# The launch of a linear-attention and MLP kernel: load order of a weight piece and an activation tile, and the place of that tile's statistics

## Chip, core and metric

One NeuronCore of a Trainium2 chip runs the whole program. The metric is the device time of one execution in microseconds; smaller is better.

## What is computed

Two identical layers on a sequence of 2048 rows of 448 features, all in float32. Each layer is an attention block without softmax and a GELU block, each behind a layer norm without gain:

```
x = x + A(layernorm(x));  x = x + B(layernorm(x))      # twice
A: q, k, v = split(x @ wqkv)        # 448 -> 3 * 448, 16 heads of 28
   phi(t) = where(t > 0, t + 1, exp(t)) + 1e-6
   kv = sum_s phi(k)[s] v[s]^T ;  z = sum_s phi(k)[s]
   o = (phi(q) kv) / (phi(q) . z + 1e-6) ;  return o @ wo
B: gelu(x @ w1 + b1) @ w2 + b2      # 448 -> 1792 -> 448
```

The change touches only the start of the first layer's attention: the layer norm of the first two tiles of x and their product with the part of wqkv that makes k.

## The kernel before

The 2048 rows are 16 tiles of 128 rows; four tiles make a block. The 448 features are cut into chunks of 128, 128, 128 and 64. Float32 products are made of two parts in the faster float32r form: each operand is a rounded `hi` and a remainder `lo`, and a product is hi·hi + hi·lo + lo·hi (L307 to L309 for a 128-row chunk, L311 and L312 for the last one, where hi and lo of the weight lie on top of one another in one piece).

A weight piece comes from HBM to a staging tile (`stage_piece`, L91, L93, L94), ScalarE (ACT) casts it to `hi` (`split_hi`, L127), and VectorE (DVE) or GpSimd (POOL) subtracts to get `lo` (`split_lo`, L134, L137). POOL does it for pieces 1 and 2 of wk and 0 and 2 of wq, DVE for the others.

A tile of x goes through these steps:

- `load_x` (L82): a DMA of 224 KB on SyncE's queue (SP).
- `stage_a`, which is `ln_stats` (L197 to L205): DVE makes the statistics (`bn_stats` L194, `bn_aggr` L200, add of epsilon L202), POOL takes the power -1/2 (L204, tile `brs`). `ln_bn` (L192) is the first of these alone.
- `stage_n` (L381): DVE normalises the tile in place (L384), and ACT copies its last 64 columns, doubled, to a tile `tail` (L388).
- `stage_b`: TensorE (PE) transposes the four chunks into one PSUM tile `tp` (L247); the fourth reads `tail`.
- For tiles 0 and 1 the split of the transposed tile is made in halves of 256 columns (`split_half`): ACT casts `XH` (L260), DVE subtracts `XL` (L262). Half 0 holds chunks 0 and 1, half 1 holds chunks 2 and 3. Half 0 of `XL` waits until both casts of `XH` are done.

The program is in a fixed order that is written by hand (`manual_schedule`): each engine takes its own instructions in the order in which the program issues them, and a waiting instruction holds up those behind it on its engine. For the start, that order is the code at L144 to L159, the calls at L912 to L919, and the string `LAUNCH` (L520), whose tokens `launch` (L534) takes one after the other: `ka1` is the cast of wk's piece 1, `kb1` its remainder, `ha0`/`hb0` the two casts of `XH` of tile 0, `la0`/`lb0` the two remainders `XL`, `n1` the normalisation of tile 1, `T1` its transposes, `K01` the products of tile 0 with wk's piece 1, `a2` the statistics of tile 2, and `Q..` the same as `K..` for wq.

On PE the launch is in this order: 11 warming products of a tile of ones (L157, each recorded as two), the transposes of tile 0, two more warming products, K00, T1, K01, K10, K11, K02, K12, K03, K13, and the same for q. On POOL, after the constants, it is: power of tile 0, power of tile 1, remainder of wk's piece 1, of piece 2, of wq's pieces 0 and 2. On SP it is: tile 0, tile 1, pieces 0 to 3 of wk (piece 3 in two halves of 112 KB), pieces 0 to 2 of wq, tile 2, piece 3 of wq, tiles 3 and on. There are eight DMA semaphores in turn, so that from the ninth DMA on SP waits for the landing of the DMA eight places ahead.

The calls before the loop over layers are, in the kernel before (L912 to L919):

```python
stage_a(0, 0)
bn = ln_bn(xt[0, 1])
stage_n(0, 0)
split_hi("k", 0, st_k)
sts[0, 1] = ln_stats(xt.pop((0, 1)), bn)
stage_b(0, 0)
warm_up(2)
```

Behind the launch comes the rest of layer 0's pass over the 16 tiles, then the product of the attention state with wv and wo, then the MLP over four blocks beside the q side of the next block, and the same for layer 1.

Of the kernel before, what the change touches and what calls it, by code (L numbers as in the profile page):

```python
# [22 lines left out]
def linear_attn_mlp_kernel(  # L23
# [15 lines left out]
    S, D = x0.shape  # L39
# [27 lines left out]
    def t448(tag, bufs, name, dt=F32):  # L67
        bufs = NH if tag == "H" else bufs
        return work.tile([128, D], dt, name=name, tag=tag, bufs=bufs)
# [8 lines left out]
    xt = {}  # L78

    def load_x(l, t):  # L80
        xt[l, t] = t448("H", 8, f"x{l}_{t}")
        sp.dma_start(xt[l, t], x_d[l][t * 128:(t + 1) * 128, :])  # L82
# [5 lines left out]
    def stage_piece(src, c, eng, s):  # L88

        if c < 3:  # L90
            eng.dma_start(s, src[c * 128:(c + 1) * 128, :])  # L91
        else:
            eng.dma_start(s[0:64], src[TL:D, :])  # L93
            eng.dma_start(s[64:128], src[TL:D, :])  # L94
        return s

    def load_kq(col, st, cs):
        src = wqkv[:, col:col + D]
        for c in cs:
            if c % 2 == 0:  # L100
                st.append(work.tile([128, 1024], F32, name="stg", tag="S", bufs=5))
                st.append(st[-1][:, 512:512 + D])
                st[-2] = st[-2][:, :D]
            stage_piece(src, c, sp, st[c])
        return st

    def stage_square(src):

        st = []
        for h in range(2):  # L110
            s = work.tile([128, 1024], F32, name="stg", tag="S", bufs=5)[:, :2 * D]
            s = s.rearrange("p (c n) -> p c n", c=2)
            if h == 0:
                sp.dma_start(s, src[:256, :].rearrange("(c p) n -> p c n", p=128))
            else:
                sp.dma_start(s[:, 0], src[256:TL, :])
                sp.dma_start(s[:64, 1], src[TL:, :])
                sp.dma_start(s[64:, 1], src[TL:, :])
            st += [s[:, 0], s[:, 1]]
        return st  # L120

    def piece(name, i):
        return t448(f"{'W' if name == 'k' else 'V'}{i}", 1, f"w{name}{i}", F32R)

    def split_hi(name, c, st):
        hi = piece(name, c if c < 3 else 6)
        act.copy(hi, st[c])  # L127
        wkq[name, c] = (hi, piece(name, 3 + c)) if c < 3 else hi

    def split_lo(name, c, st, eng):  # L130

        if c < 3:
            hi, lo = wkq[name, c]
            eng.tensor_tensor(lo, st[c], f(hi), op=OP.subtract)  # L134
        else:
            lo = wkq[name, 3][64:128]
            eng.tensor_tensor(lo, st[c][64:128], f(lo), op=OP.subtract)  # L137

    def split_kq(name, st):
        for c in range(4):  # L140
            split_hi(name, c, st)
            split_lo(name, c, st, pool if c in ((1, 2) if name == "k" else (0, 2)) else dve)

    load_x(0, 1)  # L144
    st_k = load_kq(D, [], range(4))
    st_q = load_kq(0, [], range(3))
    load_x(0, 2)
    load_kq(0, st_q, (3,))
# [6 lines left out]
    def warm_up(n):  # L155
        for i in range(n):
            pe.matmul(warm[:, :128], ones, ones, start=True, stop=True)  # L157
# [34 lines left out]
    def ln_bn(xs):  # L192
        st = work.tile([128, 6], F32, name="bst", tag="bst", bufs=3)
        dve.bn_stats(st, xs)  # L194
        return st

    def ln_stats(xs, st=None):  # L197
        st = ln_bn(xs) if st is None else st
        mv = work.tile([128, 2], F32, name="bmv", tag="bmv", bufs=3)
        dve.bn_aggr(mv, st)  # L200
        ve = work.tile([128, 1], F32, name="bve", tag="bve", bufs=3)
        dve.tensor_scalar(ve, mv[:, 1:2], 1e-5, None, op0=OP.add)  # L202
        rs = work.tile([128, 1], F32, name="brs", tag="brs", bufs=3)
        pool.tensor_tensor(rs, ve, mhalf, op=OP.pow)  # L204
        return xs, mv, rs  # L205
# [166 lines left out]
    sts = {}  # L372
# [8 lines left out]
    def stage_n(l, t):  # L381

        xs, mv, rs = sts.pop((l, t))
        dve.tensor_scalar(xs, xs, mv[:, 0:1], rs, op0=OP.subtract, op1=OP.mult)  # L384
        xns[l, t] = xs
        if t < TURNED[l]:
            d = tails[l, t] = work.tile([128, 128], F32, name="tail", tag="tail", bufs=2)
            act.copy(d.rearrange("p (u n) -> p u n", u=2), xs[:, None, TL:].to_broadcast([128, 2, 64]))  # L388
# [12 lines left out]
    def stage_b(l, t, tag="h"):  # L401
        if t < TURNED[l]:
            transpose_x(xns[l, t], tails.pop((l, t)), ("a", l, t // 4), t % 4, tag)
# [72 lines left out]
    def stage_g(l, t, acc):  # L476
# [41 lines left out]


    LAUNCH = (  # L520
        "kb0 ha0 hb0 ka1 kb1 la0 n1 lb0 K00 T1 K01 ha1 hb1 la1 lb1 ka2 kb2 K10 K11 ka3 kb3 qa0 qb0 K02 K12 K03 K13 "
        "qa1 qb1 qa2 qb2 Q00 Q10 Q01 Q11 Q02 Q12 s0 a2 kp0 qa3 qb3 kh0 n2 kl0 kp1 Q03 Q13"
    )
    PRE = 5
# [386 lines left out]

    stage_a(0, 0)  # L912
    work.tile([128, 32], F32, name="space", tag="space", bufs=1)
    bn = ln_bn(xt[0, 1])
    stage_n(0, 0)
    split_hi("k", 0, st_k)
    sts[0, 1] = ln_stats(xt.pop((0, 1)), bn)
    stage_b(0, 0)
    warm_up(2)  # L919

    for l in range(LAYERS):
        tr = SimpleNamespace(mp={})
# [34 lines left out]
        for b in range(NB):  # L957
            acc = [bank("acc", 4, f"y{j}")[:, :D] for j in range(4)]
            nxt = b + 1 < NB
            if not nxt and l + 1 < LAYERS:  # L960
                st_k = stage_square(wqkv[:, D:2 * D])
# [58 lines left out]
```

## Time and profile before

| what | us |
|---|---|
| median of 3 runs | 878.07 |
| lowest, highest | 877.53, 878.48 |
| the profiled execution | 878.62 |
| its span, first to last instruction | 876.9 |

The profiled execution is about 0.6 us above the median, and 1.7 us of it lie outside the span. In the rows of the timeline, the first number is the start in us from the span's start, the second the time that the instruction took; then come engine, line, operation, the tiles written and read, and in brackets the idle time of the engine before it with what ended it. PE's weight loads have an engine name of their own (PEld). A matmul's end is modelled and lies later than the start of the next one, so that PE's pace is read from start to start.

### The profile page before, as it was taken

The page shows a single profiled execution, that of the slowest core. Times are in us where ns is not written, and L with a number is a line of the kernel's source. Part 1 is how long each engine was busy: PE and PEld are TensorE (multiplying, and loading weights), DVE is VectorE, ACT ScalarE, POOL GpSimd, SP SyncE. Part 2 cuts the span into 40 slices and gives each one's busy share as a digit, 9 for nine tenths or more (in the row PEclk, how much of TensorE's full clock was granted, in tenths as well). Part 3 has the DMA queues.
Part 4 walks back from the last instruction along what each step waited for, and adds up shares of the span by engine and source line. Part 5 has one row for each costly group of instructions (what it writes and reads, how often), then busy time and mean ns, then how long its engine had stood idle before and what let it go on. Part 6 is the DMA issues. An engine that isn't in the chain of part 4 may idle for free.

```text
span 876.9 us, 11676 instructions
## 1 busy us (share of the span) xinstructions
PE 870.9 (99%) x4182; PEld 771.9 (88%) x4182; DVE 489.9 (56%) x953; ACT 343.5 (39%) x603; POOL 220.9 (25%) x250
## 2 busy tenths in 40 slices
PE   9999999999999999999999999999999999999998
PEld 8989888888888888888899998888888888888887
DVE  6878585658455443226467875864674473433112
ACT  5677635324223322333355665332233133223221
POOL 5566532335012102011222344120220140140000
PEclk9999999999999999999999999999999999999999
DMA  5475636623313402051145443262332413111001
GB/s 158 133 227 166 208 88 203 191 87 131 132 59 104 156 0 97 1 179 49 48 136 186 168 131 106 98 186 81 106 112 91 132 69 118 49 49 41 2 1 43
DMA packets 63482, 94.76 MB, mean 108 GB/s; under 512 B 8896, under 2 KB 58560, under 8 KB 63424
## 3 DMA queue, kind: packets, MB, share of 16 engines
q1 hardware_dynamic: 63424, 94.01, 33.5%
q8 instruction: 33, 0.54, 0.3%
q14 instruction: 25, 0.20, 0.1%
HBM read 56.17 MB, written 34.60 MB: 104 GB/s over the span
## 4 chain that ended last, share of the span: by engine, by line
PE 97%; DMA 1%; DVE 0%; POOL 0%; SPq 0%; issue 0%; ACT 0%; POOLq 0%; DVEq 0%
PE y L822 10%; PE y L820 10%; PE y L821 10%; PE hp L803 9%; PE hp L804 9%; PE hp L802 9%; PE hp L806 3%; PE hp L805 3%; PE psq L307 2%; PE psk L308 2%; PE psq L309 2%; PE psq L308 2%; PE psk L309 2%; PE G L483 2%; PE psk L307 2%; PE G L482 2%
## 5 line engine op out<-in xcount | busy, mean ns | idle before, releaser
L812 DVE TENSOR_TENSOR gl<-g,gh 128x512 fp32r<-128x512 f32 x112 | 83.1, 742 | 300.7 <-ACT gh L811 300.7
L808 ACT ACTIVATE g<-hp,b1s 128x512 f32<-128x512 f32 x112 | 77.2, 689 | 406.2 <-PE hp L806 402.7
L822 PE MATMUL y<-w2h,gl 128*128 128x448 f32 x448 | 163.7, 365 | 0.0
L821 PE MATMUL y<-w2l,gh 128*128 128x448 f32 x448 | 163.6, 365 | 0.0
L820 PE MATMUL y<-w2h,gh 128*128 128x448 f32 x448 | 163.6, 365 | 0.0
L803 PE MATMUL hp<-XH,w1l 128*128 128x512 f32 x336 | 131.5, 392 | 0.0
L802 PE MATMUL hp<-XH,w1h 128*128 128x512 f32 x336 | 131.2, 391 | 0.0
L804 PE MATMUL hp<-XL,w1h 128*128 128x512 f32 x336 | 131.2, 391 | 0.0
L204 POOL TENSOR_TENSOR brs<-bve,mhalf 128x1 f32<-128x1 f32 x64 | 39.5, 618 | 283.8 <-DVE bve L202 280.7
L820 PEld LDWEIGHTS y<-w2h,gh 128*128 128x128 f32 x448 | 84.1, 188 | 9.0
L821 PEld LDWEIGHTS y<-w2l,gh 128*128 128x128 f32 x448 | 84.1, 188 | 8.4
L822 PEld LDWEIGHTS y<-w2h,gl 128*128 128x128 f32 x448 | 84.2, 188 | 6.6
L804 PEld LDWEIGHTS hp<-XL,w1h 128*128 128x128 f32 x336 | 63.1, 188 | 14.1 <-issue 0.6
L803 PEld LDWEIGHTS hp<-XH,w1l 128*128 128x128 f32 x336 | 63.1, 188 | 11.3
L802 PEld LDWEIGHTS hp<-XH,w1h 128*128 128x128 f32 x336 | 63.1, 188 | 10.9
L811 ACT CAST gh<-g 128x512 fp32r<-128x512 f32 x112 | 69.6, 622 | 3.6
L695 POOL TENSOR_TENSOR pz<-pq,zb 128x448 f32<-128x448 f32 x32 | 36.7, 1150 | 86.4 <-DVE dn L701 75.5
L417 POOL TENSOR_TENSOR xnl<-x,xnh 128x384 fp32r<-128x384 f32 x32 | 35.1, 1097 | 70.8 <-ACT xnh L416 38.8
L297 DVE TENSOR_TENSOR XL<-sp,XH 128x512 fp32r<-128x512 f32 x50 | 44.4, 894 | 3.8 <-ACT XH L296 3.8
L806 PE MATMUL hp<-XL,w1x 128*128 128x512 f32 x112 | 43.6, 389 | 0.0
L805 PE MATMUL hp<-XH,w1x 128*128 128x512 f32 x112 | 43.6, 389 | 0.0
L764 POOL TENSOR_TENSOR x<-x,b2b 128x448 f32<-128x448 f32 x32 | 41.9, 1332 | 0.0
(146 smaller groups left out, 1563.9 us busy)
## 6 DMA issues: line engine op xcount, KB each, us to landing
x<-in_A_x_dram SPq DMA_DIRECT2D x32, 224.0 KB, 3.6
pq_d<-eq SPq DMA_DIRECT2D x32, 224.0 KB, 2.9
pq<-pq_d SPq DMA_DIRECT2D x32, 224.0 KB, 3.2
sq_m<-sq SPq DMA_DIRECT2D x14, 512.0 KB, 2.8
sp<-sq_m SPq DMA_DIRECT2D x56, 128.0 KB, 2.8
x<-x_d SPq DMA_DIRECT2D x32, 224.0 KB, 3.3
sq_a<-sq SPq DMA_DIRECT2D x12, 512.0 KB, 2.9
sp<-sq_a SPq DMA_DIRECT2D x48, 128.0 KB, 3.1
```

Source lines behind the costliest of these rows:

```text
L297: eng.tensor_tensor(lo.rearrange("p (c i n) -> p c i n", c=4, n=32), x, f(h), op=OP.subtract)
L802: pe.matmul(o, w1h[:, c, s], x.moving(x.hi, c), start=(c == 0), stop=False)
L803: pe.matmul(o, w1l[:, c, s], x.moving(x.hi, c), start=False, stop=False)
L804: pe.matmul(o, w1h[:, c, s], x.moving(x.lo, c), start=False, stop=False)
L805: pe.matmul(o, w1x[:, s], x.moving(x.hi, 3), start=False, stop=False)
L806: pe.matmul(o, w1x[:, s], x.moving(x.lo, 3), start=False, stop=True)
L808: act.activation(g, hp, AF.Gelu_apprx_tanh, bias=b1s[:, i:i + 1])
L811: act.copy(gh, g)
L812: dve.tensor_sub(gl, g, f(gh))
L820: pe.matmul(acc[j], gh[:, s], w2h[:, i], start=first, stop=False)
L821: pe.matmul(acc[j], gh[:, s], w2l[:, i], start=False, stop=False)
L822: pe.matmul(acc[j], gl[:, s], w2h[:, i], start=False, stop=last)
```

## The change

Three edits.

1. Load order on SP: tile 0, then wk's piece 0, then tile 1, then wk's pieces 1 to 3; the rest as before.
2. Before the loop, the cast of wk's piece 0 stands ahead of tile 0's normalisation with its copy of the tail. On ACT the order becomes: cast of piece 0, `tail` of tile 0, both halves of `XH`, cast of piece 1 and so on as before. The statistics of tile 1 leave this place; in `LAUNCH` they come back as `a1`, behind `la0`. On DVE the order becomes: statistics of tile 0, its normalisation, remainder of wk's piece 0, half 0 of `XL`, the three instructions of tile 1's statistics, half 1 of `XL`, normalisation of tile 1. On POOL nothing changes places: the power of tile 1 is still ahead of the remainder of wk's piece 1.
3. The two warming products behind tile 0's transposes are removed. PE's order is otherwise the same.

In `LAUNCH`, `ka1 kb1` move behind `lb0`, which changes no engine's order except as told above.

```diff
+    st_k = load_kq(D, [], range(1))
     load_x(0, 1)
-    st_k = load_kq(D, [], range(4))
+    load_kq(D, st_k, range(1, 4))
     st_q = load_kq(0, [], range(3))
...
     LAUNCH = (
-        "kb0 ha0 hb0 ka1 kb1 la0 n1 lb0 K00 T1 K01 ha1 hb1 la1 lb1 ka2 kb2 K10 K11 ka3 kb3 qa0 qb0 K02 K12 K03 K13 "
+        "kb0 ha0 hb0 la0 a1 lb0 ka1 kb1 n1 K00 T1 K01 ha1 hb1 la1 lb1 ka2 kb2 K10 K11 ka3 kb3 qa0 qb0 K02 K12 K03 K13 "
...
     stage_a(0, 0)
     work.tile([128, 32], F32, name="space", tag="space", bufs=1)
-    bn = ln_bn(xt[0, 1])
+    split_hi("k", 0, st_k)
     stage_n(0, 0)
-    split_hi("k", 0, st_k)
-    sts[0, 1] = ln_stats(xt.pop((0, 1)), bn)
     stage_b(0, 0)
-    warm_up(2)
```

## Prediction

> **What bounds the kernel now.** I read the page first, then PE's waits over the whole span, then the timeline of the launch. The page's busy shares:
>
> ```profile
> PE 870.9 (99%) x4182; PEld 771.9 (88%) x4182; DVE 489.9 (56%) x953; ACT 343.5 (39%) x603; POOL 220.9 (25%) x250
> ```
>
> PE never rests outside a few places, so a change at the start can only move the moment from which PE runs without gaps. PE's waits name those places:
>
> ```profile
> PE warm L157 <- DVE ones L152: 1.1, 1, 1.1
> PE psq L307 <- DVE eq L321: 0.5, 1, 0.5
> PE psk L307 <- ACT XH L260: 0.5, 1, 0.5
> ```
>
> The first and the third lie in the launch. The second is late:
>
> ```profile
> 47.64 0.47 PE L307 MATMUL psq<-wq,XH 128*128 128x448 f32 x1 [0.48 <-DVE eq L321]
> ```
>
> It belongs to tiles that are loaded and split long after the launch, by engines that are themselves led by PE; I let it move along with the rest, and keep its 0.48 as the most that it could give back. Now the launch:
>
> ```profile
> 0.80 0.86 SPq L82 DMA_DIRECT2D x<-in_A_x_dram  x2
> ...
> 1.70 1.38 SPq L91 DMA_DIRECT2D stg<-in_A_wqkv_dram  x3
> ...
> 3.42 0.63 DVE L194 BATCH_NORM_STATS2 bst<-x 128x6 f32<-128x448 f32 x1 [2.35 <-DMA x<-in_A_x_dram]
> ...
> 4.37 0.62 DVE L194 BATCH_NORM_STATS2 bst<-x 128x6 f32<-128x448 f32 x1
> 4.53 0.55 POOL L204 TENSOR_TENSOR brs<-bve,mhalf 128x1 f32<-128x1 f32 x1 [2.17 <-DVE bve L202]
> 5.12 0.51 DVE L384 TENSOR_SCALAR x<-x,bmv,brs 128x448 f32<-128x448 f32 x1
> ...
> 5.66 0.30 ACT L388 COPY tail<-x 128x128 f32<-128x128 f32 x1 [3.58 <-DVE x L384]
> ...
> 6.16 0.27 PE L247 MATMUL tp<-ident,tail 128*128 128x128 f32 x1
> ...
> 6.44 0.56 ACT L127 CAST wk<-stg 128x448 fp32r<-128x448 f32 x1 [0.48 <-DMA stg<-in_A_wqkv_dram]
> 6.91 0.64 ACT L260 CAST XH<-tp 128x256 fp32r<-128x256 f32 x2
> ...
> 7.33 0.47 PE L307 MATMUL psk<-wk,XH 128*128 128x448 f32 x1 [0.45 <-ACT XH L260]
> 7.44 0.58 ACT L127 CAST wk<-stg 128x448 fp32r<-128x448 f32 x1
> 7.58 0.42 DVE L262 TENSOR_TENSOR XL<-tp,XH 128x256 fp32r<-128x256 f32 x1
> ...
> 7.92 0.50 DVE L384 TENSOR_SCALAR x<-x,bmv,brs 128x448 f32<-128x448 f32 x1
> ...
> 8.10 1.33 POOL L134 TENSOR_TENSOR wk<-stg,wk 128x448 fp32r<-128x448 f32 x1 [1.55 <-ACT wk L127]
> ...
> 8.46 0.30 ACT L388 COPY tail<-x 128x128 f32<-128x128 f32 x1 [0.45 <-DVE x L384]
> ...
> 8.48 0.55 PE L247 MATMUL tp<-ident,x 128*128 128x128 f32 x3
> ...
> 9.18 0.65 ACT L260 CAST XH<-tp 128x256 fp32r<-128x256 f32 x2 [0.42 <-PE tp L247]
> 9.48 0.19 PEld L308 LDWEIGHTS psk<-wk,XH 128*128 128x128 f32 x1 [0.42 <-POOL wk L134]
> ...
> 9.71 1.05 ACT L127 CAST wk<-stg 128x448 fp32r<-128x448 f32 x2
> ...
> 10.37 1.16 POOL L134 TENSOR_TENSOR wk<-stg,wk 128x448 fp32r<-128x448 f32 x1 [0.94 <-ACT wk L127]
> ...
> 11.58 0.19 PEld L308 LDWEIGHTS psk<-wk,XH 128*128 128x128 f32 x1 [0.34 <-POOL wk L134]
> ```
>
> The last wait of the launch is the one at 11.58: K02's second product needs the remainder of wk's piece 2, which POOL starts at 10.37. Follow it back: piece 2's cast (9.71) stands on ACT behind the casts of tile 1's XH (9.18), these need T1 (8.48), T1 needs tile 1 normalised (7.92), and that stands on DVE right behind XL (7.58), which follows XH (6.91), which stands on ACT behind the cast of piece 0 (6.44), which waited for its DMA. So **tile 1's normalisation, n1, is on the path**; its statistics were made early (4.37) in DVE's idle time and cost nothing. Everything behind 11.58 is dense on PE: what n1 is late, the kernel is late.
>
> **The change part by part.**
>
> *Load order.* Four answers of the DMA view, one per issue (tile 0, tile 1, piece 0, piece 1 of wk), in us to landing:
>
> ```profile
> x<-in_A_x_dram SPq DMA_DIRECT2D x1, 224.0 KB, 2.6
> ...
> x<-in_A_x_dram SPq DMA_DIRECT2D x1, 224.0 KB, 2.7
> ...
> stg<-in_A_wqkv_dram SPq DMA_DIRECT2D x1, 224.0 KB, 4.7
> ...
> stg<-in_A_wqkv_dram SPq DMA_DIRECT2D x1, 224.0 KB, 5.1
> ```
>
> With issues near 0.8, 1.2, 1.7 and 2.2, they land near 3.4, 3.9, 6.4 and 7.3. The first piece of wk lands 2.5 behind its neighbour, and the change moves it by one place. If only the place counted, it would land at 3.9; if the place counted nothing, at 6.4. One place is worth 0.5 (3.4 to 3.9) to 0.9 (6.4 to 7.3) elsewhere in this list; I take 0.6: **piece 0 lands at 5.8**, as the row it is nearest to is its own, a strided load. Tile 1 then lands where piece 0 does now, near 6.4, and is needed at 8.0: hidden. wk's pieces 1 to 3 and wq keep their places; the DMA that waits eight places behind (wq's piece 2, free to go from 5.5) now waits for 5.8 instead of 3.9, and its landing, due much later, does not show.
>
> *The cast of piece 0 ahead of the tail.* This adds a wait: on ACT, tile 0's tail and XH now stand behind the landing of piece 0. Cast 5.82; the next ACT instruction starts 0.47 later (6.44 to 6.91), so the tail starts at 6.29 instead of 5.66 and ends at 6.59; from a tail's end to XH it is 0.42 (8.76 to 9.18). **XH at 7.01, now 6.91: +0.10.** The cast that left the place ahead of XH came back ahead of the tail. Landing at 5.25 or sooner would give XH at 6.46, -0.45; landing at 6.4, +0.7. K00's products follow XH and XL by the same steps as now; the remainder of piece 0 is made on DVE by 7.0, ahead of XL.
>
> *Statistics behind XL.* XL starts 0.67 behind XH (6.91 to 7.58): 7.68; the next DVE instruction 0.34 later (7.58 to 7.92): statistics at 8.02. From there to a normalisation it takes 1.70, by tile 0's rows (3.42 to 5.12): n1 at 9.72, where it would have been at 8.02. **+1.70**, in full on the path. Half 1 of XL (0.42) fits into POOL's power (0.55) and hides.
>
> *POOL's next instruction beside n1.* Behind tile 1's power on POOL stands the remainder of wk's piece 1. Its cast will have ended near 8.1 (7.27 for the second XH, cast at 7.54, 0.58), so that POOL takes it the moment the power ends, just as n1 starts on DVE. The trace has that meeting:
>
> ```profile
> 21.53 1.02 POOL L417 TENSOR_TENSOR xnl<-x,xnh 128x384 fp32r<-128x384 f32 x1
> 21.60 1.20 DVE L384 TENSOR_SCALAR x<-x,bmv,brs 128x448 f32<-128x448 f32 x1 [0.20 <-POOL brs L204]
> ...
> 422.13 2.41 POOL L764 TENSOR_TENSOR x<-x,b2b 128x448 f32<-128x448 f32 x2
> 422.20 1.33 DVE L384 TENSOR_SCALAR x<-x,bmv,brs 128x448 f32<-128x448 f32 x1 [0.73 <-POOL brs L204]
> ```
>
> Both times POOL started 0.07 ahead, and the normalisation took 1.20 and 1.33 instead of 0.51; it ended 0.25 behind the POOL instruction (22.55 to 22.80; in the second case 0.2, with half of 2.41 for one). Here POOL starts at 8.02 + 1.66 - 0.03 = 9.65 and takes 1.16 (the row at 10.37): 10.81, n1 ends at 11.06. Undisturbed it would end at 10.23: **+0.83**. Bounds: 0, if n1 starts first; 0.83 plus a little, if blocked. Both rows with this meeting went one way. [...]
>
> *From n1 on.* n1 ends at 11.06 instead of 8.43: +2.63. T1 at 11.12, XH of tile 1 at 11.81, cast of piece 2 at 12.34, POOL at 13.00, K02's second product at 14.21, all by today's steps. K01 no longer waits for POOL (piece 1 is done at 10.81), but that wait was not the last one.
>
> *Two warming products less.* They stand at 6.3 to 6.9, where PE has nothing else: 0 on the path. What they may cover is the clock, the first rival.
>
> **Sum**: 0.10 + 1.70 + 0.83 = **+2.63**. The profiled execution was 878.62: 881.25. It stands 0.55 above the median, so against 878.07: **880.7**.
>
> **The rivals.**
>
> *The clock falls back.* Weight loads of the warming products, then two slices of the windows view of the end (us of PE, PEld, DVE, ACT and POOL, then granted clock):
>
> ```profile
> 1.12 4.68 PEld L157 LDWEIGHTS warm<-ones 128*128 128x128 f32 x22 [1.12 <-DVE ones L152]
> ...
> 6.16 0.53 PEld L157 LDWEIGHTS warm<-ones 128*128 128x128 f32 x4
> ```
>
> ```profile
> 873.00:874.00 1.00, 0.12 (x1) 0.00 (x0) 0.85 (x2) 0.00 (x0) 0.00 (x0) 1.00 0.99 380
> ...
> 876.00:876.90 0.90, 0.00 (x0) 0.00 (x0) 0.00 (x0) 0.00 (x0) 0.00 (x0) 0.54 0.00 0
> ```
>
> The loads came 0.21 apart for some 4.5 us, then 0.13: PE begins at about half pace. At the end the clock was granted for about 3 us after the last product, then fell to half. In the changed kernel PE has, between 7.0 and 11.1, only K00's three products: about as empty, and fuller by those. If the clock falls, the work from T1 on runs at half pace for up to the 4.5 us that the first rise took, a loss between 0 and 2.2; part falls into PE's waits ahead of 14.21. I take 1.0: 881.7. [...]
>
> *The piece lands early, or n1 wins over POOL.* Landing by 5.25: 0.55 less, 880.15. n1 ahead of POOL: 0.83 less, 879.9. For the first speaks that tile 1 lands at 3.9 in that place; against it, that both pieces of wk in those rows take 4.7 and more.
>
> *The path is another: not slower.* The page's own chain follows PE's wait at 9.48 back to the landing of wk's piece 1 (POOL at 8.10, cast at 7.44). If that landing bounds the launch and n1 has cover, the change costs nothing: 878.1. It would need POOL to take piece 1 ahead of tile 1's power, and PE to have work ahead of T1; by the order of both engines neither is so. The deciding point is n1's end: up to 8.5 nothing is lost.
>
> *The piece lands no earlier*: +0.6 more, 881.3.
>
> **How the numbers follow.** Chances: forecast 0.48, clock 0.25, early or n1 first 0.15, no earlier 0.05, another path 0.07. A measurement of this kernel can tell about 0.2%, 1.76 us, from no change: 879.83 is the edge. The forecast, the clock and the late landing lie over it, but for 0.02; of the early case 0.09 lies over it and 0.06 below; the other path is within; faster is given 0.03, taken from these, for a late wait that goes away, as that of 47.64, together with a launch that loses nothing. So slower 0.84, same 0.13, faster 0.03. The range reaches from 879.5 (early landing with some of the 0.48 given back) to 882.2 (the clock with half of its bound above my value); left out are the other path and the outer ends, under 0.2.
>
> **What would show it.** Right: cast of piece 0 near 5.8 behind its DMA, tail of tile 0 near 6.3; tile 1's statistics near 8.0; n1 from 9.7, lasting over 1.1 beside L134 on POOL; T1 near 11.1; K02's second product near 14.2, and PE dense behind it. Wrong: n1 of 0.5; T1 ahead of 10; products more than 0.3 apart behind T1 with no wait between them (the clock); a wait at 47 us that has gone or doubled.

## The result, and the profile after

| what | us |
|---|---|
| before, median of 6 runs (lowest, highest) | 878.28 (877.53, 878.91) |
| after, median of 6 runs (lowest, highest) | 882.24 (880.24, 883.57) |
| after divided by before, 95% interval | 1.0039 (1.0029 to 1.0049) |
| after, the profiled execution; its span | 881.74; 880.0 |

The changed kernel is slower by about 4 us. The forecast was 880.7 and its range ended at 882.2, 0.04 below the median. Its six executions are not alike. Each comes with the mean clock that TensorE was granted, and the two go together: 880.24 at 1.000; 881.08 and 881.74 at 0.998; 882.73 and 882.75 at 0.996; 883.57 at 0.995. The 81 executions of the kernel before that were run beside the experiments show 0.999 or 1.000.

PE's busy share is the same 99%. In its waits, T1's wait for tile 1 normalised (`x`, now L385, since helper lines moved down by one) is new and the wait of 0.48 at 47.64 has gone:

```profile
PE 872.2 (99%) x4178; PEld 773.3 (88%) x4178; DVE 490.2 (56%) x953; ACT 343.6 (39%) x603; POOL 220.6 (25%) x250
```

```profile
PE tp L248 <- DVE x L385: 2.4, 1, 2.4
PE warm L158 <- DVE ones L153: 1.1, 1, 1.1
PE psk L308 <- ACT XH L261: 0.5, 1, 0.5
```

The DMA view, for one issue after another (tile 0, wk's piece 0, tile 1, wk's piece 1), gives the time from issue to landing. With the issues at 0.80, 1.24, 1.70 and 2.18 they land near 3.4, 3.9, 6.4 and 7.4:

```profile
x<-in_A_x_dram SPq DMA_DIRECT2D x1, 224.0 KB, 2.6
...
stg<-in_A_wqkv_dram SPq DMA_DIRECT2D x1, 224.0 KB, 2.7
...
x<-in_A_x_dram SPq DMA_DIRECT2D x1, 224.0 KB, 4.7
...
stg<-in_A_wqkv_dram SPq DMA_DIRECT2D x1, 224.0 KB, 5.2
```

That is the list of before (2.6, 2.7, 4.7, 5.1) with the names exchanged. In these two profiles the landing went by the place in the queue, not by what was loaded. The timeline of the launch:

```profile
1.12 5.06 PE L158 MATMUL warm<-ones 128*128 128x128 f32 x22 [1.12 <-DVE ones L153]
...
3.96 0.56 ACT L127 CAST wk<-stg 128x448 fp32r<-128x448 f32 x1 [1.88 <-DMA stg<-in_A_wqkv_dram]
...
5.68 0.30 ACT L389 COPY tail<-x 128x128 f32<-128x128 f32 x1 [1.16 <-DVE x L385]
...
5.97 0.85 PE L248 MATMUL tp<-ident,x 128*128 128x128 f32 x3
...
7.07 0.65 ACT L261 CAST XH<-tp 128x256 fp32r<-128x256 f32 x2 [1.08 <-PE tp L248]
...
7.75 0.43 DVE L263 TENSOR_TENSOR XL<-tp,XH 128x256 fp32r<-128x256 f32 x1 [1.57 <-ACT XH L261]
...
8.09 0.62 DVE L195 BATCH_NORM_STATS2 bst<-x 128x6 f32<-128x448 f32 x1
...
9.19 0.55 POOL L205 TENSOR_TENSOR brs<-bve,mhalf 128x1 f32<-128x1 f32 x1 [4.09 <-DVE bve L203]
9.71 1.13 POOL L134 TENSOR_TENSOR wk<-stg,wk 128x448 fp32r<-128x448 f32 x1
9.78 1.31 DVE L385 TENSOR_SCALAR x<-x,bmv,brs 128x448 f32<-128x448 f32 x1 [0.34 <-POOL brs L205]
...
11.14 0.90 PE L248 MATMUL tp<-ident,x 128*128 128x128 f32 x3 [2.45 <-DVE x L385]
...
13.48 1.15 POOL L134 TENSOR_TENSOR wk<-stg,wk 128x448 fp32r<-128x448 f32 x1 [2.64 <-ACT wk L127]
...
15.01 0.36 PE L309 MATMUL psk<-wk,XH 128*128 128x448 f32 x1
```

Read from the bottom: K02's second product starts at 15.01 (before 11.58), n1 lasts 1.31 beside POOL's L134 (9.71), and the statistics start at 8.09, behind XL. POOL's piece 2 is ready at 14.63, so that the last product is no longer held by POOL: PE itself is late. The windows view shows why; the third figure from the end is the granted clock:

```profile
9.00:10.00 1.00, 0.00 (x0) 0.00 (x0) 0.66 (x3) 0.00 (x0) 0.81 (x2) 1.00 1.02 337
10.00:11.00 1.00, 0.00 (x0) 0.00 (x0) 1.00 (x1) 0.00 (x0) 0.84 (x1) 0.83 0.94 255
11.00:12.00 1.00, 0.86 (x5) 0.86 (x5) 0.09 (x1) 0.30 (x1) 0.00 (x0) 0.50 1.04 321
12.00:13.00 1.00, 1.00 (x5) 0.91 (x4) 0.03 (x1) 0.70 (x3) 0.00 (x0) 0.50 0.87 310
13.00:14.00 1.00, 1.00 (x5) 0.87 (x4) 0.82 (x3) 1.00 (x3) 0.52 (x1) 0.50 0.31 117
14.00:15.00 1.00, 1.00 (x6) 0.94 (x5) 1.00 (x1) 1.00 (x3) 1.00 (x2) 0.96 0.00 0
```

PE has nothing from 8.7 to 11.1; the clock falls at 10.7 and is back at 14.1, and T1, K01 and K10 run at half pace (products 0.37 apart, from 12.43 to 12.80, and 0.20 once it is back, from 14.81 to 15.01). The first rise was late in this execution as well: the trace's clock record begins at 7.25 (before: 5.67; the view writes 1.00 for the time ahead of a first record). Tile 0's three transposes take 0.64 from 5.97 to 6.61 there, where they take 0.38 at full pace (5.70 to 6.08 in the first experiment below), and they started late, since the warming products ran at half pace until 6 (their weight loads some 0.22 apart: 22 in 4.77 us).

### The profile page after: what moved, and what is told of

It is laid out like the page before. It is cut to its first block, busy times and chain, and to the rows that moved or that the text cites. A ratio compares the mean times of both kernels' runs of the same rounds, so it can differ in the third digit from the quotient of the medians.

```text
span 880.0 us, 11669 instructions
## 1 busy us (share of the span) xinstructions
PE 872.2 (99%) x4178; PEld 773.3 (88%) x4178; DVE 490.2 (56%) x953; ACT 343.6 (39%) x603; POOL 220.6 (25%) x250
## 4 chain that ended last, share of the span: by engine, by line
PE 98%; DVE 1%; issue 1%; DMA 0%; POOL 0%; DVEq 0%; POOLq 0%
PE y L823 10%; PE y L822 10%; PE y L821 10%; PE hp L804 9%; PE hp L805 9%; PE hp L803 9%; PE hp L806 3%; PE hp L807 3%; PE psk L309 2%; PE psk L308 2%; PE G L483 2%; PE psq L310 2%; PE psk L310 2%; PE psq L308 2%; PE G L484 2%; PE G L485 2%
```

## Experiments

The theory: three things make up the loss, and the load order is none of them. They are the place of tile 1's statistics, the meeting of n1 with POOL's remainder of wk's piece 1, and the clock, which falls because PE is left nearly empty ahead of T1. The rivals: the clock falls because the two warming products are gone; the loss comes from a late landing; or the longer n1 has another cause than POOL. `w6` stands for six warming products (twelve as recorded), put into PE's order between K00 and T1 by a token of its own in `launch`.

This table gathers the runs; T1 and K02's second product are the start times in the profiled execution of each, and the fifth column counts the executions whose clock share (the mean granted clock over the span) was below 0.999. One stretch of 3.41 us at half pace takes 0.002 off the share of 880 us; the fall behind the last product of a kernel takes off at most 0.001 in these profiles.

| kernel | T1 | K02's 2nd | median | clock fell | ratio (95%) |
|---|---|---|---|---|---|
| before | 8.48 | 11.58 | 878.28 | 0 of 81 | 1 |
| after | 11.14 | 15.01 | 882.24 | 5 of 6 | 1.0039 (1.0029 to 1.0049) |
| e1_fill | 10.47 | 13.56 | 880.45 | 0 of 8 | 1.0025 (1.0015 to 1.0036) |
| e2_pool_first | 9.81 | 12.90 | 880.85 | 8 of 10 | 1.0029 (1.0019 to 1.0039) |
| e7_pool_and_fill | 9.79 | 12.89 | 880.05 | 0 of 9 | 1.0022 (1.0012 to 1.0031) |
| e4_stats_early | 9.10 | 12.20 | 880.01 | 7 of 11 | 1.0017 (1.0008 to 1.0026) |
| e11_stats_early_fill | 9.44 | 12.54 | 879.84 | 0 of 11 | 1.0012 (1.0003 to 1.0021) |
| e10_warm_kept | 10.40 | 14.49 | 881.25 | 3 of 5 | 1.0032 (1.0020 to 1.0045) |
| e5_dve_piece1 | 8.75 | 11.85 | 878.06 | 0 of 11 | 1.0001 (0.9992 to 1.0010) |
| e12_n1_first | 8.87 | 12.27 | 878.57 | 2 of 11 | 1.0004 (0.9995 to 1.0013) |
| e3_no_warm | 7.94 | 11.04 | 878.58 | 0 of 11 | 1.0000 (0.9992 to 1.0009) |
| e6_act_queue | 8.87 | 11.97 | 878.62 | 0 of 11 | 1.0006 (0.9997 to 1.0015) |
| e9_cast_behind | 8.57 | 12.04 | 878.86 | 0 of 11 | 1.0007 (0.9998 to 1.0016) |

The kernel before, run beside them, had medians of 878.30 (e1 to e4), 878.15 (e5, e6, e7, e9) and 878.52 (e10 to e12), and none of its 81 executions fell below 0.999. Single executions of one kernel spread by 1 to 3 us, so differences below some 0.8 in a median, about half the width of the intervals, are not read. T1 and K02 come from one execution each, and with them the moment at which the clock first rose and the one at which the third load landed; both differ from execution to execution.

### e1_fill: work for PE ahead of T1

```diff
-        "kb0 ha0 hb0 la0 a1 lb0 ka1 kb1 n1 K00 T1 K01 ha1 hb1 la1 lb1 ka2 kb2 K10 K11 ka3 kb3 qa0 qb0 K02 K12 K03 K13 "
+        "kb0 ha0 hb0 la0 a1 lb0 ka1 kb1 n1 K00 w6 T1 K01 ha1 hb1 la1 lb1 ka2 kb2 K10 K11 ka3 kb3 qa0 qb0 K02 K12 K03 K13 "
...
+            elif name == "w":
+                warm_up(j)
```

> The changed kernel with six warming products put on PE between K00 and T1, where PE was empty for 2.4 us; nothing else is moved. Theory (the clock falls because PE is nearly empty between 7 and 11 us): with the gap filled the clock stays full behind its first rise, T1 still starts near 11.1 (tile 1's normalisation is untouched), its four transposes come 0.11 apart and not 0.21, K02's second product starts near 14.2 and not 15.0, and the time is that of the one undisturbed execution of the changed kernel, 880.2, at most 880.8, with executions less than 1 us apart. Rival (the clock has nothing to do with that gap, or its fall costs nothing): the time stays at 882.2 with executions 3 us apart.

The timeline of this kernel:

```profile
6.39 0.65 ACT L261 CAST XH<-tp 128x256 fp32r<-128x256 f32 x2 [0.42 <-PE tp L248]
...
7.42 0.62 DVE L195 BATCH_NORM_STATS2 bst<-x 128x6 f32<-128x448 f32 x1
...
7.86 1.50 PE L158 MATMUL warm<-ones 128*128 128x128 f32 x12
...
9.04 1.13 POOL L134 TENSOR_TENSOR wk<-stg,wk 128x448 fp32r<-128x448 f32 x1
9.10 1.31 DVE L385 TENSOR_SCALAR x<-x,bmv,brs 128x448 f32<-128x448 f32 x1 [0.33 <-POOL brs L205]
...
10.47 0.55 PE L248 MATMUL tp<-ident,x 128*128 128x128 f32 x3 [1.10 <-DVE x L385]
...
13.56 0.47 PE L309 MATMUL psk<-wk,XH 128*128 128x448 f32 x1
```

The clock was kept in all eight executions and the median is 1.8 below that of the changed kernel, though the products do nothing that is used. This is also the launch as it looks when the clock has risen in time: XH at 6.39, 0.5 sooner than before, because piece 0 lands early. From T1 to K02's second product it is 3.09, and the delay is 13.56 - 11.58 = 1.98; the median lies 2.15 above that of the kernel before. T1 stands at 10.47 and not near 11.1 as expected, because the clock rose earlier here (4.73) than in the changed kernel's profile (7.25); the executions spread by 1.7, not by less than 1.

### e10_warm_kept: only the two warming products put back

```diff
     stage_b(0, 0)
+    warm_up(2)
```

> The changed kernel with its two warming products put back behind tile 0's transposes; nothing else differs. Theory A (it is the emptiness of PE between K00 and T1, some 2.4 us, that lets the clock fall, and the two products behind tile 0's transposes lie too early to fill it): the clock share still falls under 0.999 in more than half of the executions, the median stays within 0.8 of 882.2, and in an execution that keeps its clock the time is near 880.2. Rival B (removing the two products is what lost the clock): the share stays at 0.999 or above in all executions and the median is 880.2 to 880.5.

```profile
10.40 0.60 PE L248 MATMUL tp<-ident,x 128*128 128x128 f32 x3 [2.45 <-DVE x L385]
...
14.49 0.37 PE L309 MATMUL psk<-wk,XH 128*128 128x448 f32 x1
```

```profile
7.00:8.00 1.00, 0.89 (x3) 0.23 (x2) 0.96 (x2) 0.57 (x1) 0.00 (x0) 1.00 1.05 272
8.00:9.00 1.00, 0.00 (x0) 0.00 (x0) 0.67 (x3) 0.00 (x0) 0.55 (x2) 1.00 0.96 344
...
10.00:11.00 1.00, 0.60 (x5) 0.58 (x5) 0.35 (x1) 0.30 (x1) 0.10 (x1) 0.88 1.02 249
11.00:12.00 1.00, 1.00 (x5) 0.91 (x4) 0.07 (x1) 0.74 (x3) 0.00 (x0) 0.50 1.05 317
```

In this profile the trace's clock record has the full clock from 3.94, XH stood at 6.33, and the clock still fell at 10.77 and came back at 14.18: 3.41 at half pace. From T1 to K02's second product it took 4.09 instead of 3.09, so **one fall costs 1.0 us here**. The clock fell in three of five executions. The emptiness ahead of T1 (PE idle for 2.45 us here) was enough; whether the two products lower the chance of a fall can't be told from three of five against five of six. The rival is refuted in its strong form only. The median, 881.25, was 0.15 lower than the theory's lower bound of 881.4, and the two executions that kept the clock, 880.61 and 881.03, lie above its 880.2; the kernel before took 878.52 beside them.

### e2_pool_first and e7_pool_and_fill: POOL takes piece 1 ahead of tile 1's power

```diff
+        "kb0 ha0 hb0 ka1 kb1 la0 a1 lb0 n1 K00 T1 K01 ha1 hb1 la1 lb1 ka2 kb2 K10 K11 ka3 kb3 qa0 qb0 K02 K12 K03 K13 "
```

The line replaced is the one of the changed kernel, here and below. e7 is this with `w6` between `K00` and `T1`.

> The changed kernel with the remainder of wk's piece 1 on POOL ahead of tile 1's power instead of behind it. Theory (the normalisation of tile 1 took 1.31 because POOL's remainder started just ahead of it): the power comes some 0.2 later, the normalisation takes 0.51, ends near 10.5 instead of 11.09, and T1 starts near 10.55 instead of 11.14; the time falls by 0.5 to 0.6 from 882.2, to 881.6, as the clock can still fall. Rival (the normalisation is slow of itself at that place): it stays at 1.3, T1 moves to 11.3, and the time is 882.4.

> The changed kernel with both mendings: the remainder of wk's piece 1 on POOL ahead of tile 1's power, and six warming products between K00 and T1. Theory (meeting on POOL and clock are two separate terms that add): tile 1's normalisation takes 0.5, T1 near 9.8, the clock stays full in every execution, the time is that of the undisturbed executions of the kernel with POOL's order alone, 879.5, that is 1.2 over the kernel before. Rival (the fill costs as much as it saves, or the clock's fall was another's doing): 880.5 or more.

The timeline of e2:

```profile
7.56 1.13 POOL L134 TENSOR_TENSOR wk<-stg,wk 128x448 fp32r<-128x448 f32 x1 [2.49 <-ACT wk L127]
8.65 0.56 POOL L205 TENSOR_TENSOR brs<-bve,mhalf 128x1 f32<-128x1 f32 x1
9.24 0.52 DVE L385 TENSOR_SCALAR x<-x,bmv,brs 128x448 f32<-128x448 f32 x1 [0.50 <-POOL brs L205]
...
9.81 0.55 PE L248 MATMUL tp<-ident,x 128*128 128x128 f32 x3 [1.81 <-DVE x L385]
...
12.90 0.48 PE L309 MATMUL psk<-wk,XH 128*128 128x448 f32 x1
```

n1 takes 0.52 instead of 1.31: the meeting is what lengthens it, by 0.79. (T1 came earlier than the expected 10.55, which was reckoned from the changed kernel's late XH at 7.07; here it stood at 6.37.) Since the power now stands behind piece 1, n1 starts 0.14 later, and 0.66 is left at T1 against e1. Alone it gains less than that in the median, as the clock still falls in eight of ten; the two executions that kept it took 879.55 and 879.57, the other eight 881.4 in the median. With the filler, e7 keeps the clock throughout, but its median of 880.05 is 1.9 above the kernel before where its launch is 1.31 late, and lies between the 879.5 of the theory and the 880.5 of the rival. Its launch is that of e2 (K02's second product at 12.89 and 12.90), so that what is left lies elsewhere. Its profile has a wait of 0.42 at 141.69 that the others don't show; the profiled execution is the slowest of the nine, and that this wait explains the rest was not tested.

### e4_stats_early and e11_stats_early_fill: the statistics ahead of XL

```diff
+        "kb0 ha0 hb0 a1 la0 lb0 ka1 kb1 n1 K00 T1 K01 ha1 hb1 la1 lb1 ka2 kb2 K10 K11 ka3 kb3 qa0 qb0 K02 K12 K03 K13 "
```

e11 is this with four warming products (`w4`) between `K00` and `T1`.

> The changed kernel with tile 1's statistics ahead of XL's first half instead of behind it; load order, cast and removed warming products stay. Theory (the place of the statistics is the largest term): tile 1 lands at 6.4, its power ends near 8.1, the normalisation starts near 8.1, still meets POOL's remainder of piece 1 and ends near 9.3, T1 near 9.4 instead of 11.1; PE is empty for less than 1.5 us, so that the clock stays; the time is 1.0 over the kernel before, 879.3. Rival (the load order is what costs, since tile 1 lands 2.5 later): T1 stays behind 10.5 and the time over 881.

> Tile 1's statistics ahead of XL, as tried alone before (T1 at 9.10, clock share under 0.999 in 7 of 11 executions, median 880.0, and 879.3 in the four that kept the clock), and now four warming products (eight as recorded, about 1.0 us) between K00 and T1. Theory A (what that kernel lost over the 879.3 was the clock, and 1.1 us of idle PE ahead of T1 suffices to lose it): share 0.999 or above in all executions, T1 near 9.1, median 879.0 to 879.5. Rival B (the loss comes from elsewhere, as from a late wait or the chip's spread): shares under 0.999 remain, or the median stays at 880.

The timeline of e4:

```profile
6.04 0.62 DVE L195 BATCH_NORM_STATS2 bst<-x 128x6 f32<-128x448 f32 x1
...
7.67 1.13 POOL L134 TENSOR_TENSOR wk<-stg,wk 128x448 fp32r<-128x448 f32 x1
7.73 1.31 DVE L385 TENSOR_SCALAR x<-x,bmv,brs 128x448 f32<-128x448 f32 x1
...
9.10 0.55 PE L248 MATMUL tp<-ident,x 128*128 128x128 f32 x3 [1.13 <-DVE x L385]
...
12.20 0.48 PE L309 MATMUL psk<-wk,XH 128*128 128x448 f32 x1
```

n1 starts at 7.73 instead of 9.10: 1.37. Not all of the 1.68 that lie between statistics and n1 in e1 (7.42 to 9.10) came back, because two things now hold n1 to about the same moment: the power, 7.15 to 7.70, and the second half of XL, which stands ahead of n1 on DVE here. I had not expected the clock to fall with PE idle for only 1.13 ahead of T1, and it did in seven of eleven executions (880.2 in their median; 879.3 in the four others). The profiled execution, from which the 1.13 is read, is one of the four that kept it. With eight recorded products in that gap it fell in none of eleven. The median of e11 was then 879.84, above the 879.0 to 879.5 of the theory; its profiled execution had the clock rise at 6.36 and T1 0.34 later than e4, and the kernel before was 0.2 slower beside it. The filler kept the clock, but against e4's 880.01 the median did not move by anything that can be told: in that the rival was right, and that holding the clock gains time in this kernel is not shown.

### e5_dve_piece1 and e12_n1_first: nothing meets n1

```diff
+        "kb0 ha0 hb0 a1 la0 lb0 ka1 n1 kb1 K00 T1 K01 ha1 hb1 la1 lb1 ka2 kb2 K10 K11 ka3 kb3 qa0 qb0 K02 K12 K03 K13 "
...
-                split_lo(name[0], j, st_k if name == "kb" else st_q, pool if tok in ("kb1", "kb2", "qb0", "qb2") else dve)
+                split_lo(name[0], j, st_k if name == "kb" else st_q, pool if tok in ("kb2", "qb0", "qb2") else dve)
```

e12 differs from it in the order `la0 n1 lb0 ka1 kb1` behind `a1`.

> The changed kernel with tile 1's statistics ahead of XL's first half, and the remainder of wk's piece 1 made by DVE behind tile 1's normalisation instead of by POOL; load order, cast and removed warming products stay. Theory (what is left of the load order costs little: tile 1's normalisation then waits for its landing near 6, plus 1.7): the normalisation takes 0.5 from 7.7 to 8.1 on, T1 near 8.3 to 8.7, PE empty for under 0.6 us ahead of it, clock full, the time within 0.5 of the kernel before: 878.3 to 878.8. Rival (the load order itself costs, by tile 1's late landing): 879.3 or more.

> The changed kernel's load order, tile 1's statistics ahead of XL, its normalisation between the halves of XL as in the kernel before, and the remainder of wk's piece 1 on VectorE behind both halves of XL, so that nothing meets n1. Theory A (three causes account for all of the loss: place of the statistics, meeting on POOL, clock): power ends near 7.7, n1 at 7.75 and 0.5 long, T1 near 8.3, K02's second product near 11.4, the clock keeps its share, median 877.5 to 878.0; that is at most 0.5 below the kernel before and can hardly be told from it. Rival B (K01 waits for the remainder of piece 1 on VectorE, done only near 9.3, and that wait takes the place of T1's): K02's second product near 11.8 and 878.1 as without this step.

The timeline of e5:

```profile
5.97 0.62 DVE L195 BATCH_NORM_STATS2 bst<-x 128x6 f32<-128x448 f32 x1
...
8.19 0.51 DVE L385 TENSOR_SCALAR x<-x,bmv,brs 128x448 f32<-128x448 f32 x1
8.61 0.62 DVE L134 TENSOR_TENSOR wk<-stg,wk 128x448 fp32r<-128x448 f32 x1
...
8.75 0.55 PE L248 MATMUL tp<-ident,x 128*128 128x128 f32 x3 [0.29 <-DVE x L385]
```

With the changed load order, the early cast and no warming products behind tile 0, but the statistics early and piece 1's remainder on DVE, the whole loss is gone: 1.0001 (0.9992 to 1.0010). So **the new load order costs nothing that these runs can tell** (the interval reaches to 0.9 us), and mending the three causes together is enough. e12 went on to put n1 between the halves of XL, as the kernel before has it. It gained nothing:

```profile
6.60 0.63 DVE L195 BATCH_NORM_STATS2 bst<-x 128x6 f32<-128x448 f32 x1 [0.39 <-DMA x<-in_A_x_dram]
...
9.65 0.63 DVE L134 TENSOR_TENSOR wk<-stg,wk 128x448 fp32r<-128x448 f32 x1 [0.50 <-ACT wk L127]
```

Tile 1 landed at 6.6 in this execution, so that its statistics waited 0.39 for it: with the statistics this early, a late landing of tile 1 does reach n1 (8.30 instead of the expected 7.75). Then `n1` brings its copy of the tail on ACT (8.85), the cast of piece 1 stood behind that copy (9.05), its remainder on DVE came at 9.65, K01 waited for it, and K02's second product came at 12.27; the clock fell in two of eleven. The rival was right in kind, though the remainder was done later (10.28) than it had it (9.3). No version beats the kernel before by more than the measurement can tell.

### e3_no_warm, e6_act_queue, e9_cast_behind: parts of the change on the kernel before

e3 leaves out `warm_up(2)` from the kernel before, and nothing else. e6 has ACT issue the load of wk's piece 0:

```diff
+    st_k = load_kq(D, [], (0,), act)
     load_x(0, 1)
-    st_k = load_kq(D, [], range(4))
+    load_kq(D, st_k, range(1, 4))
```

e9 puts the cast of piece 0 behind XH, its remainder behind n1, and K00 behind T1:

```diff
-        "kb0 ha0 hb0 ka1 kb1 la0 n1 lb0 K00 T1 K01 ha1 hb1 la1 lb1 ka2 kb2 K10 K11 ka3 kb3 qa0 qb0 K02 K12 K03 K13 "
+        "ha0 hb0 ka0 ka1 kb1 la0 n1 kb0 lb0 T1 K00 K01 ha1 hb1 la1 lb1 ka2 kb2 K10 K11 ka3 kb3 qa0 qb0 K02 K12 K03 K13 "
...
-    split_hi("k", 0, st_k)
```

> The kernel before with its two warming products behind tile 0's transposes taken away, nothing else. Theory (they are not needed as long as T1 starts at 8.5): no difference, within 0.3 us of the kernel before, clock full in every execution once risen. Rival (these two products hold the clock up, and their removal is what the change lost): some executions at a clock of 0.998 or less, 1 to 2 us slower in the median.

> The kernel before with wk's piece 0 issued by ACT instead of SP, so that the first three loads are tile 0 and tile 1 on SP and piece 0 on ACT, all issued near 1 us; nothing else. Theory (the third load on one engine's queue is the late one): piece 0 lands by 4.6, tile 1 near 3.9, XH starts at 6.4, T1 near 8.0, the launch is 0.5 shorter than in the profiled kernel before, where piece 0 landed at 6.4; the time 0 to 0.5 below 878.3. Rival (the third load of all is late, whoever issues it, or two queues take from one another): one of the three lands near 6, or tile 0 later than 3.4, and the time is 878.3 or more.

> The kernel before with the cast of wk's piece 0 behind both halves of XH on ACT, its remainder behind tile 1's normalisation on DVE, and T1 ahead of K00 on PE, so that the landing of piece 0 no longer stands ahead of tile 1's chain. Theory (the path is tile 1's chain and not piece 0's products): XH at 6.4 and T1 at 8.0 whenever piece 0 lands, K02's second product near 11.1 as in the executions where it lands early, the time 0 to 0.5 below 878.3. Rival (K00's products matter): the wait moves to K00's second product and T1's gain is lost there, 878.3 or more.

Without the two warming products the kernel before is unchanged (1.0000, 0.9992 to 1.0009) and keeps its clock in eleven of eleven: T1's weight load has only 0.23 to wait there. Its profile also shows that the launch of the kernel before moves with the landing of piece 0, the third load: here it landed at 5.7 and not at 6.4, XH stood at 6.36 and not at 6.91, and K02's second product at 11.04 and not at 11.58. In e6, from the DMA view, ACT's load of piece 0 (first row) and SP's of tile 0 start together at 0.80:

```profile
stg<-in_A_wqkv_dram ACTq DMA_DIRECT2D x1, 224.0 KB, 3.5
x<-in_A_x_dram SPq DMA_DIRECT2D x1, 224.0 KB, 3.3
```

With two queues, all of the first three loads had landed by 4.7, but tile 0, which starts the whole chain, came 0.7 later than with all loads on SP's queue (statistics at 4.13 instead of 3.42). No gain was left. In e9 the cast of piece 0 left the path to XH, K00 moved behind T1, and that gave no gain either: the clock rose only at 6.76 in the profiled execution, XH came at 7.00, and from T1 to K02's second product it took 3.47 instead of 3.09, with K00's products in between, as the rival had it.

## Why the prediction was right or wrong

**The reading of before: right.** n1 sets the launch, and what it is late, the kernel is late. T1 to K02's second product was forecast as 3.09 (11.12 to 14.21) and is 3.09 in e1 and e2, where the clock holds.

**Load order: wrong.** I took the landing at 5.8, because the row nearest to it was its own, a strided load. It landed at 3.94, the lower end that I had kept (3.9). Strided or not, the second load landed at 3.8 to 4.0 and the third at 5.6 to 6.6 in the traces with all these loads on one queue. The step "+0.10" for XH is then -0.52 (6.39 in e1 against 6.91). The "lands early" rival had 0.55 for it, with a chance that was too small. In the profiled execution XH came at 7.07, near the 7.01 forecast, by another cause: a clock that rose only at 7.25. That n1 (9.78 for 9.72) and T1 (11.14 for 11.12) stand there where they were forecast is therefore luck. And the gain of 0.52 is against a profile in which piece 0 landed at 6.4; against e3, where it landed at 5.7 in its old place, XH gains nothing (6.36).

**Statistics behind XL, +1.70: right.** XL to statistics 0.34, statistics to n1 1.69 (8.09 to 9.78). Statistics ahead of XL gave 1.37 of it back (e4).

**POOL beside n1, +0.83: right.** n1 lasted 1.31, and 0.79 of it is gone without the meeting. POOL's remainder, which started first (9.71), took 1.13, as in e2, where it stood ahead of the power and did not meet n1; n1, from 9.78 on, ended 0.25 behind it (10.84 to 11.09), which is less than the 0.52 that n1 took in e2. The meeting in the other order is in the rows of before: there n1 started first (7.92) and kept its 0.50, and POOL's remainder, started at 8.10, took 1.33 instead of 1.16.

**Two warming products, 0 on the path: right as far as tried.** On the kernel before they cost and give nothing (e3); put back into the changed kernel they did not hold the clock (e10).

**The clock: right as a rival, wrong as a chance.** I gave it 0.25 and a price of 1.0. The price is that of one fall (4.09 - 3.09 in e10; in the changed kernel's profile 0.78, from 15.01 and 11.14 + 3.09 = 14.23), though the half pace lasted 3.41 us and not the 4.5 that I took. But it fell in five of six executions, and the lower shares of 0.996 and 0.995 with 2.5 and 3.3 us over the execution that kept it point to more than one half-paced stretch in those; which stretches these were no trace here shows. The step that failed is "about as empty, and fuller by those": K00's three products were counted as cover, and they were not enough. The sign that was named for it, products more than 0.3 apart behind T1 with no wait between them, is in the profile (12.43 and 12.80). Two profiles show the length of the half pace, 3.41 us in both; and executions of one and the same kernel lost the clock or kept it (seven and four of e4's eleven). In both profiles PE was mostly but not wholly empty in the 3.41 us ahead of the fall: in e10, 7.36 to 10.77 held K00's last product and the first transposes, and PE was busy for 0.90 us of it; in the changed kernel, 7.25 to 10.67 held K00's three products, 1.14 us.

**The sum.** Without the clock, and with the clock risen in time, the launch is 1.98 late (e1, against the profile of before), and the one execution of the changed kernel that kept its clock took 880.24, 1.96 above the kernel before. It is 1.70 + 0.79 less the 0.5 of the earlier landing. On top come about 2.0 in the median for the clock: 882.24. Between the two profiled executions the difference is 3.12 (881.74 less 878.62): the launch is 3.43 later (15.01 against 11.58), and the wait of 0.48 at 47.64 is gone. The forecast of 880.7 thus lies 1.5 below the median: its load-order term was 0.6 too high, and the clock, which is half of the 4.0 that were lost, was left out of the sum and stood among the rivals. The ends of the range don't follow from the sums beside them either: 880.15 less 0.48 is 879.67 and not 879.5, and the clock with half of its bound above my value is 882.3 and not 882.2.

## What to carry over

In a launch like this one, count PE's busy time ahead of each wait: here the unfilled wait of 2.45 us ahead of T1 was followed in two profiles by a stretch at half pace, which cost 0.8 and 1.0 us on top of it. When a statistic is moved behind something, follow it to the engine that consumes it, and look at what POOL starts just ahead of that engine's instruction (0.79 us on n1 here). The landing times of the queued loads went by place here, so exchanging two loads exchanged their times.

## What the runs showed of the hardware

- The two falls of the clock that are recorded in a launch came 3.41 and 6.83 us behind its rise (7.25 to 10.67 in the changed kernel, 3.94 to 10.77 in e10), and 3.41 us later it was back (14.08 and 14.18).
- At the full clock a float32r product of 448 columns followed the one before it by 0.20 us (14.81 to 15.01 in the changed kernel). A float32 warming product of 128 columns, recorded as two, took about 0.25 (six in 1.50 us in e1).
- In these runs the length of one wait did not decide: the clock fell in 7 of 11 executions of e4, whose profile has PE idle for 1.13 us in one piece, and in none of 11 of e9, with 1.17. What went with the falls is the emptiest stretch of 3.41 us in the launch of each profile (from 3.9 us on, by the windows view). PE was busy in it for 0.90 us in the changed kernel (7.74 to 11.15) and in e10, 1.16 in e2, 1.76 in e4 and 2.00 in e12, which are the five kernels whose clock fell; and for 2.17 in e9, 2.25 in e1 and 2.48 or more in all others, whose clock did not. It is one profile for each kernel, and those of e2, e4 and e12 kept the clock, so this is no measured threshold.
- In these traces the first rise of the clock came between 3.94 and 7.25 us with the same eleven warming products from 1.1 on. Where it came behind 6.3, some or all of tile 0's transposes ran at half pace and XH came 0.4 to 0.7 later (6.80 in e11, 6.84 in e5 and 7.07 in the changed kernel, against 6.39 in e1).
- In these traces, with all loads on SP's queue, the third landed 1.7 to 2.6 us behind the second, issued 0.46 apart. In e6, with the first load of wk on ACT's queue, the last of the first three landed 0.4 behind the one before it, and tile 0 landed 0.7 later than in the kernel before (4.1 instead of 3.4).
